# An attention and token-mixing MLP kernel: order of small loads, due phases of DVE steps, SBUF places and held pairs

## The chip, the core and the metric

The kernel runs on one core of one Trainium2 chip, as one launch. The core has TensorE (PE in the profile, its weight loads PEld), VectorE (DVE), ScalarE (ACT), GpSimd (POOL) and SyncE (SP), which issues the kernel's DMAs from one queue in program order. The metric is the time of one execution on the device in microseconds, as a median of several runs.

## The reference

`x` is 2048 rows (S) of 512 (D), everything in fp32. Two branches are mixed row by row with a gate:

```python
def _A_ref(x, wqkv, wo):                 # attention, H = 32 heads of Dh = 16
    qkv = (x @ wqkv).reshape(B, S, 3, H, Dh).transpose(2, 0, 3, 1, 4)
    q, k, v = qkv[0], qkv[1], qkv[2]
    p = softmax(einsum("bhqd,bhkd->bhqk", q, k) * Dh ** -0.5, axis=-1)
    o = einsum("bhqk,bhkd->bhqd", p, v)
    return o.transpose(0, 2, 1, 3).reshape(B, S, D) @ wo

def _B_ref(x, w1, b1, w2, b2):           # MLP across the tokens, F = 1792
    h = layernorm(x)
    u = gelu(einsum("bsd,sf->bdf", h, w1) + b1)
    return (einsum("bdf,fs->bds", u, w2) + b2).transpose(0, 2, 1)

g = sigmoid((x * gate_w).sum(-1, keepdims=True))
return g * _A_ref(...) + (1 - g) * _B_ref(...)
```

## The kernel before

**Stages.** Dense products are made in split precision: each fp32 operand becomes a high and a low part, and three matmuls (hi x hi, hi x lo, lo x hi) are added. The v, q and k projections come first, then the MLP's first layer (`layer`, with `gelu` on DVE and ACT; its last step is L438, `u_lo<-gu`). From about 305 us on runs the attention loop, whose instructions on all five engines stand in the order in which the code gives them (`manual_schedule`). A short end stage finishes the output projection.

**The loop.** There are 32 groups: 2 halves of the queries by 16 pairs of heads. Each group has four phases (`PHASES`), 128 in all, numbered `p`; `ph` is the phase within its group. A phase has 16 score matmuls (L876) on 64 rows of the TensorE array, into PSUM banks named s (one bank) or t (two). Between them, on the other 64 rows, stand up to 14 matmuls of dense work (L885): the MLP's second layer in groups 0 to 22, then the output projection of the first query half and parts of the second half's. Four scores are copied by DVE to an SBUF tile `pe` (L893), which ACT exponentiates at once at the end of the phase (L913). Six are exponentiated singly from PSUM (L897, tiles `p1`) and six as three pairs of banks (L906, tiles `p2` with four buffers). Then follow the av matmuls (L776, `apply_v`), which multiply the exps by v and, in the same matmuls, by a column that makes the softmax denominators r. DVE copies or adds their result to the group's tile `ot` (L798 add, L800 copy) and so frees the av bank.

**Held pairs.** The 16 exps of a phase are used in pairs: six in `TURNS`, the last of them (14, 15), and two in `HELD`, the `pe` pairs, whose av matmuls are made in the next phase. In `ph` 0, the previous group's held pairs come first and close that group: `store` sends its o (L765) and r (L767) to DRAM with four DMAs each. Also in `ph` 0, under a condition on which query blocks the turns cover, the pair (14, 15) is held over too. The condition is there because the result in `ot` can be added for one head or for both, but not for half of one.

**Order of the small work in a phase.** At the head of a phase, SP issues the next group's queries in `ph` 0 (`load_q`, 8 DMAs of 64 KB, L502) and keys in `ph` 1 (`load_k`, 6 DMAs of 128 KB, L502). After them come the entries of `calls` for that phase, and DVE steps recorded in `later` run after the phase's evacuations and before its `ot` addition (L923). What goes through `calls` and `later`:

- `invert(half, k, pairs, at)`: four groups fill one 128-row block k of the attention output. In the phase after their last store it loads the block's denominators (`inv<-r`, L615), takes maximum and reciprocal on DVE (L618, L619) in phase `at`, and writes them back in the next phase (`ri<-inv`, L623). The eight inversions lie in `ph` 1 of groups 4, 8, 12, 16, 20, 24, 28 and 31.
- `fetch_o(half, k, places, ats)`: loads block k of o (`e<-o`, L633) and its reciprocals spread over the rows of each head (`o_sum<-ri`, L634), and multiplies, copies the high part and subtracts for the low part on DVE, in the phases `ats`. `o_sum` has two buffers. The first half's four fetches are issued in phases 92, 92, 94 and 95 (group 23), the second half's first two in 99 and 102.
- `load_wo`, `load_wq`, and the loads of finished MLP rows (`row<-bp`).

**SBUF.** Places are given to pools from one side in the order in which they are opened: o, the stacks `stk` (two buffers of keys, two of queries), `ot` with the small tiles `inv`, `row` and `token`, then `pt` with the exps. A tile waits for the release of whatever lay there before; in the loop's first phases these are the MLP's tiles. In bytes of a partition the stacks begin at 69120 (where the normalized rows were), and `pt` at 104480.

Of the kernel before, what the change touches and what calls it, by code (L numbers as in the profile page):

```python
# [58 lines left out]
def gated_mix(ctx: ExitStack, tc: tile.TileContext, a_x, a_wqkv, a_wo, b_w1, b_b1, b_w2, b_b2, gate_w, out):  # L59
# [419 lines left out]
    o_pool = ctx.enter_context(tc.tile_pool(name="o", bufs=1, reuse_waits="tile"))  # L479
    att_ctx = ExitStack()  # L480
    stk = att_ctx.enter_context(tc.tile_pool(name="stk", bufs=2, reuse_waits="tile"))
    out_pool = att_ctx.enter_context(tc.tile_pool(name="ot", bufs=2, reuse_waits="tile"))
# [49 lines left out]
    ri_d = [[dram.tile([P // DH, QW], F32, name=f"ri{h}{k}") for k in range(ND)] for h in range(2)]  # L532
    ptp_ctx = ExitStack()
    ptp = ptp_ctx.enter_context(tc.tile_pool(name="pt", bufs=2, reuse_waits="tile"))
    psum_ctx = ExitStack()
# [28 lines left out]
    def call(at, *what):  # L564
        calls.setdefault(at, []).append(what)
# [31 lines left out]
    def place(n):  # L597
        return end.tile([P, QW], F32R, name=f"e{n}")

    def load_wq(at):  # L600
        wq.extend(place(n).rearrange("p (i c) -> p i c", i=2) for n in (4, 5))
        raw = end.tile([P, QW], F32, name="o_sum", bufs=2).rearrange("p (i c) -> p i c", i=2)
        nc.gpsimd.memset(raw, 0.0)
# [5 lines left out]

    def invert(half, k, pairs, at):  # L610

        n = pairs * 2
# [14 lines left out]
    def fetch_o(half, k, places, ats, pairs=4):  # L627

        n = pairs * 2
        rb = end.tile([P, QW], F32, name="o_sum", bufs=2)[: n * DH]  # L630
        hi, lo = (place(i)[: n * DH] for i in places)
# [74 lines left out]
    for half in range(2):  # L706
        for k in range(ND):
            pairs = 3 if half and k == ND - 1 else 4
            p0 = PHASES * (half * NP + 4 * k + pairs)
            call(p0 + 1, invert, half, k, pairs, p0 + 1)  # L710
    p0 = 2 * at
    call(p0, open_end)
    call(p0, fetch_o, 0, 0, (0, 1), (p0 + 1, p0 + 1, p0 + 1))
    call(p0, fetch_o, 0, 1, (2, 3), (p0 + 1, p0 + 2, p0 + 2))
    call(p0 + 2, fetch_o, 0, 2, (4, 5), (p0 + 2, p0 + 2, p0 + 3))
    call(p0 + 3, fetch_o, 0, 3, (6, 7), (p0 + 3, p0 + 3, p0 + 3))
    at += 2
    for t in range(NH):
        at = put_output(t, 3 * ND, at)
    p1 = PHASES * (NP + 2 * 4) + 3  # L720
    call(p1, fetch_o, 1, 0, (8, 9), (p1 + 1, p1 + 2, p1 + 2))
    call(p1 + 3, fetch_o, 1, 1, (10, 11), (p1 + 4, p1 + 5, p1 + 5))
    p2 = PHASES * (NP + 3 * 4) + 2
# [83 lines left out]
    with tc.manual_schedule(engines=engines):  # L807
# [11 lines left out]
        for p in range(LAST + 1):  # L819
            grp, ph = divmod(p, PHASES)  # L820
            second = ph % 2
            if ph == 0:
                at = [[0, 0], [0, 0]]
                if grp + 1 < NG:
                    qt[grp + 1] = load_q(grp + 1)
            if ph == 1 and grp + 1 < NG:
                kt[grp + 1] = load_k(grp + 1)
            for what, *args in calls.get(p, ()):
                what(*args)
            if not second:  # L830
# [94 lines left out]
            turns, now_held = ([tuple(units[n] for n in pair) for pair in pairs] for pairs in (TURNS, HELD))  # L925
            spare = share[2]
            if ph == 0:
                if held:
                    apply_v(av, grp - 1, held, final=True)
                    spare = share[3]  # L930
                    av = psum.tile([P, NB], F32, name=f"s{spare}")
                whole = {qb for pair in turns for i, _, qb, _ in pair if i}
                if len(whole) == 1:
                    now_held = now_held + turns[-1:]
                    turns = turns[:-1]
                apply_v(av, grp, turns)
# [11 lines left out]
    psum_ctx.close()  # L948

    ptp_ctx.close()  # L950


    with (
# [14 lines left out]

        parts, whole = place(6), end.tile([P, QW], F32, name="o_sum", bufs=2)
        sums, hi, lo = (column_halves(x) for x in (whole[:, :NB], parts[:, :NB], parts[:, NB:]))  # L970
# [140 lines left out]
```

## Time and profile before

| | us |
|---|---|
| runs: median (lowest to highest, 3 runs) | 1345.89 (1345.78 to 1346.16) |
| the profiled execution | 1346.58 |
| its span, from first to last instruction | 1344.8 |
| busy: PE / DVE / ACT / POOL | 1296.8 / 670.2 / 1094.2 / 178.6 |
| mean granted TensorE clock | 0.981 |

A row of the costliest groups reads: line, engine, operation, output<-input (partitions x elements, type) xcount, then busy us in all, mean ns of one, and after the second bar the idle time of that engine just before such an instruction with what ended most of it. A row of the list of waits reads: engine, tile and line that waits, <- what it waits for: us in total, times, longest. A row of the timeline reads: start, length, engine, line, operation, tile<-tiles, count, and in brackets the idle time before it with its releaser. "SPq" is the issuing of DMAs on SP. A run of equal instructions is one row with its count, and a window cuts such runs at its ends.

### The profile page before, as it was taken

The page shows a single profiled execution, that of the slowest core. Times are in us where ns is not written, and L with a number is a line of the kernel's source. Part 1 is how long each engine was busy: PE and PEld are TensorE (multiplying, and loading weights), DVE is VectorE, ACT ScalarE, POOL GpSimd, SP SyncE. Part 2 cuts the span into 40 slices and gives each one's busy share as a digit, 9 for nine tenths or more (in the row PEclk, how much of TensorE's full clock was granted, in tenths as well). Part 3 has the DMA queues.
Part 4 walks back from the last instruction along what each step waited for, and adds up shares of the span by engine and source line. Part 5 has one row for each costly group of instructions (what it writes and reads, how often), then busy time and mean ns, then how long its engine had stood idle before and what let it go on. Part 6 is the DMA issues. An engine that isn't in the chain of part 4 may idle for free.

```text
span 1344.8 us, 33141 instructions
## 1 busy us (share of the span) xinstructions
PE 1296.8 (96%) x13278; PEld 850.9 (63%) x13278; DVE 670.2 (50%) x1143; ACT 1094.2 (81%) x1537; POOL 178.6 (13%) x272
## 2 busy tenths in 40 slices
PE   9999999998999899999999999999999799998998
PEld 7888888875666566656656665666565356655554
DVE  5775471366444445444544453444444646454555
ACT  3453353358999899989989998999899789998994
POOL 0210344560111011101101101110110000000000
PEclk9999999999999899999999999999999899998999
DMA  3596633245343333424433333333224645333422
GB/s 127 155 319 259 221 100 99 87 102 107 78 90 77 74 74 79 88 51 88 84 64 67 76 72 59 78 86 80 59 53 95 136 97 120 83 86 85 84 45 77
DMA packets 92463, 133.20 MB, mean 99 GB/s; under 512 B 16182, under 2 KB 55244, under 8 KB 89229
## 3 DMA queue, kind: packets, MB, share of 16 engines
q1 hardware_dynamic: 91724, 129.94, 40.2%
q8 instruction: 108, 1.77, 0.6%
q10 hardware_dynamic: 576, 1.05, 0.2%
q14 instruction: 55, 0.44, 0.1%
HBM read 97.00 MB, written 33.93 MB: 97 GB/s over the span
## 4 chain that ended last, share of the span: by engine, by line
PE 82%; ACT 7%; DMA 5%; SPq 3%; issue 2%; DVE 1%; DVEq 0%; ACTq 0%
PE av L776 24%; PE s L876 18%; PE acc L416 11%; PE t L876 10%; PE acc L73 9%; PE s L776 4%; DMA inv<-r 3%; PE dn L885 3%; ACT p L897 2%; ACT p L906 2%; ACT pe L913 2%; SPq L502 1%; SPq L767 1%; DMA o_sum<-ri 1%; SPq L765 1%
## 5 line engine op out<-in xcount | busy, mean ns | idle before, releaser
L897 ACT ACTIVATE p<-s 128x512 f32<-128x512 f32 x768 | 397.5, 656 | 54.0 <-PE s L876 29.0
L876 PE MATMUL s<-qs,ks 64*128 64x512 f32 x1344 | 345.5, 408 | 35.3 <-DVE ot L800 17.1
L906 ACT ACTIVATE p<-t 128x1024 f32<-128x1024 f32 x352 | 349.8, 1139 | 0.4 <-PE t L876 0.2
L876 PEld LDWEIGHTS s<-qs,ks 64*128 64x128 f32 x1344 | 232.7, 186 | 140.5 <-issue 73.7
L893 DVE COPY pe<-s 128x512 f32<-128x512 f32 x512 | 317.7, 683 | 6.9 <-PE s L876 6.1
L776 PE MATMUL av<-p,v 128*32 128x256 f32 x4832 | 279.3, 380 | 0.0
L798 DVE TENSOR_TENSOR ot<-av,ot 128x512 f32<-128x512 f32 (+1 forms) x128 | 73.0, 571 | 386.7 <-PE av L776 386.6
L913 ACT ACTIVATE pe<-pe 128x2048 f32<-128x2048 f32 x129 | 260.8, 2024 | 0.0
L776 PEld LDWEIGHTS av<-p,v 128*32 128x32 f32 x4832 | 156.9, 111 | 106.6 <-issue 3.6
L876 PE MATMUL t<-qs,ks 64*128 64x512 f32 x704 | 189.4, 457 | 3.9 <-ACT p L897 0.2
L885 PE MATMUL dn<-u_lo,w_hi 64*128 64x512 f32 x430 | 177.7, 413 | 0.0
L885 PE MATMUL dn<-u_hi,w_lo 64*128 64x512 f32 x430 | 176.8, 411 | 0.0
L885 PE MATMUL dn<-u_hi,w_hi 64*128 64x512 f32 x428 | 175.5, 410 | 0.0
L66 POOL TENSOR_TENSOR w_lo<-w_raw,w_hi 128x512 fp32r<-128x512 f32 (+1 forms) x126 | 148.7, 1187 | 124.5 <-ACT w_hi L65 107.8
L876 PEld LDWEIGHTS t<-qs,ks 64*128 64x128 f32 x704 | 98.0, 190 | 86.7 <-ACT p L897 78.3
L776 PE MATMUL av<-pe,v 128*32 128x256 f32 x2048 | 144.0, 400 | 0.3 <-ACT pe L913 0.3
L889 POOL MEMSET token<- 1x1 f32 x124 | 11.4, 92 | 920.5 <-PE dn L885 791.6
L65 ACT CAST w_hi<-w_raw 128x512 fp32r<-128x512 f32 (+1 forms) x67 | 38.1, 569 | 79.6 <-PE acc L416 58.7
L776 PEld LDWEIGHTS av<-pe,v 128*32 128x32 f32 x2048 | 54.9, 112 | 60.7 <-ACT p L897 25.1
L416 PE MATMUL acc<-h_hi,w_hi 128*128 128x512 f32 x224 | 87.1, 389 | 0.0
L416 PE MATMUL acc<-h_lo,w_hi 128*128 128x512 f32 x224 | 87.1, 389 | 0.0
L416 PE MATMUL acc<-h_hi,w_lo 128*128 128x512 f32 x224 | 87.1, 389 | 0.0
(148 smaller groups left out, 1514.6 us busy)
## 6 DMA issues: line engine op xcount, KB each, us to landing
w_raw<-in_B_w_dram SPq DMA_DIRECT2D x96, 256.0 KB
ks<-kp SPq DMA_DIRECT2D x192, 128.0 KB
qs<-qp SPq DMA_DIRECT2D x256, 64.0 KB
qp<-pc SPq DMA_DIRECT2D x16, 768.0 KB
x<-in_A_x_dram SPq DMA_DIRECT2D x32, 256.0 KB
kp<-pc SPq DMA_DIRECT2D x16, 512.0 KB
w_raw<-in_B_w_dram SPq DMA_DIRECT2D x32, 128.0 KB
bp<-row SPq DMA_DIRECT2D x16, 256.0 KB
```

Of the source, the lines that this page charges most:

```text
L65: copy(hi, src)
L66: return sub(lo, src, hi.bitcast(F32), ALU.subtract)
L73: nc.tensor.matmul(ps, a, b, start=start and n == 0, stop=stop and n == last)
L416: nc.tensor.matmul(p, a, b, start=first and k == 0, stop=last and k == 2)
L776: nc.tensor.matmul(av[32 * j : 32 * (j + 1), i * QC : (i + 1) * QC], v_flat[:, v_at : v_at + 32], pt[:, h * QC : (h + 1) * QC], start=n == ...
L798: nc.vector.tensor_tensor(x, y, x, ALU.add)
L876: nc.tensor.matmul(s, kt[grp][rows_i, c * P : (c + 1) * P], qt[grp][rows_i, qb * NB : (qb + 1) * NB], start=True, stop=True,)
L885: mm = nc.tensor.matmul(ps, a[half], b[half], start=begin and not second, stop=last and bool(second))
L893: nc.vector.tensor_copy(pt, s)
L897: nc.scalar.activation(pt, s, AF.Exp, scale=SCALE)
L906: nc.scalar.activation(pt, twos[low, low + 1], AF.Exp, scale=SCALE)
L913: nc.scalar.activation(x, x, AF.Exp, scale=SCALE)
```

## The change

- `calls` of a phase are made at its head, ahead of `load_q` and `load_k`; before, they came after them.
- `invert`'s load stays in the same phase, and its DVE steps and the write back come two phases later, except for the second half's blocks 2 and 3 (groups 28 and 31).
- All four fetches of the first half are issued in phase 92; `o_sum` has three buffers. Their DVE phases stay. The second half's first two are issued in phases 99 and 103 (99 and 102 before), their DVE steps in 101, 102, 102 and 105, 106, 106 (100, 101, 101 and 103, 104, 104 before).
- The pool `pt` is opened ahead of `stk` and `ot`. In bytes of a partition `pt` now begins at 69120, the stacks at 114176 (keys 114176 and 122368, queries 130560 and 134656), and `ot` at 138752. In the first layer the bytes 130816 to 139008 held the gelu tiles `gu` and `gs`.
- In every phase but the last of a group, the pair (14, 15) is held over to the next phase, if the pairs that remain (with the held ones of the phase before, outside `ph` 0) cover both query blocks of each head that they touch.

```diff
--- before.py
+++ after.py
@@ -478,6 +478,7 @@
     bp_d = [dram.tile([P, D], F32, name=f"bp{t}") for t in range(NS)]
     o_pool = ctx.enter_context(tc.tile_pool(name="o", bufs=1, reuse_waits="tile"))
     att_ctx = ExitStack()
+    ptp = att_ctx.enter_context(tc.tile_pool(name="pt", bufs=2, reuse_waits="tile"))
     stk = att_ctx.enter_context(tc.tile_pool(name="stk", bufs=2, reuse_waits="tile"))
     out_pool = att_ctx.enter_context(tc.tile_pool(name="ot", bufs=2, reuse_waits="tile"))
     QW = 2 * NB
@@ -530,8 +531,6 @@
     o_d = [[dram.tile([P, QW], F32, name=f"o{h}{k}") for k in range(ND)] for h in range(2)]
     r_d = [[dram.tile([P // DH, QW], F32, name=f"r{h}{k}") for k in range(ND)] for h in range(2)]
     ri_d = [[dram.tile([P // DH, QW], F32, name=f"ri{h}{k}") for k in range(ND)] for h in range(2)]
-    ptp_ctx = ExitStack()
-    ptp = ptp_ctx.enter_context(tc.tile_pool(name="pt", bufs=2, reuse_waits="tile"))
     psum_ctx = ExitStack()
     ps_dn = psum_ctx.enter_context(tc.tile_pool(name="ps_dn", bufs=1, space=PSUM, reuse_waits="tile"))
     o_parts = {}
@@ -599,7 +598,7 @@
 
     def load_wq(at):
         wq.extend(place(n).rearrange("p (i c) -> p i c", i=2) for n in (4, 5))
-        raw = end.tile([P, QW], F32, name="o_sum", bufs=2).rearrange("p (i c) -> p i c", i=2)
+        raw = end.tile([P, QW], F32, name="o_sum", bufs=3).rearrange("p (i c) -> p i c", i=2)
         nc.gpsimd.memset(raw, 0.0)
         for j in range(4):
             nc.sync.dma_start(
@@ -609,6 +608,7 @@
 
     def invert(half, k, pairs, at):
 
+
         n = pairs * 2
         w = QW // DH
         t = out_pool.tile([P, w], F32, name="inv")[: n * DH]
@@ -627,7 +627,7 @@
     def fetch_o(half, k, places, ats, pairs=4):
 
         n = pairs * 2
-        rb = end.tile([P, QW], F32, name="o_sum", bufs=2)[: n * DH]
+        rb = end.tile([P, QW], F32, name="o_sum", bufs=3)[: n * DH]
         hi, lo = (place(i)[: n * DH] for i in places)
         raw = lo.bitcast(F32)
         nc.sync.dma_start(raw, o_d[half][k][: n * DH])
@@ -706,20 +706,20 @@
     for half in range(2):
         for k in range(ND):
             pairs = 3 if half and k == ND - 1 else 4
-            p0 = PHASES * (half * NP + 4 * k + pairs)
-            call(p0 + 1, invert, half, k, pairs, p0 + 1)
+            p0 = PHASES * (half * NP + 4 * k + pairs) + 1
+            call(p0, invert, half, k, pairs, p0 + (0 if half and k > 1 else 2))
     p0 = 2 * at
     call(p0, open_end)
     call(p0, fetch_o, 0, 0, (0, 1), (p0 + 1, p0 + 1, p0 + 1))
     call(p0, fetch_o, 0, 1, (2, 3), (p0 + 1, p0 + 2, p0 + 2))
-    call(p0 + 2, fetch_o, 0, 2, (4, 5), (p0 + 2, p0 + 2, p0 + 3))
-    call(p0 + 3, fetch_o, 0, 3, (6, 7), (p0 + 3, p0 + 3, p0 + 3))
+    call(p0, fetch_o, 0, 2, (4, 5), (p0 + 2, p0 + 2, p0 + 3))
+    call(p0, fetch_o, 0, 3, (6, 7), (p0 + 3, p0 + 3, p0 + 3))
     at += 2
     for t in range(NH):
         at = put_output(t, 3 * ND, at)
     p1 = PHASES * (NP + 2 * 4) + 3
-    call(p1, fetch_o, 1, 0, (8, 9), (p1 + 1, p1 + 2, p1 + 2))
-    call(p1 + 3, fetch_o, 1, 1, (10, 11), (p1 + 4, p1 + 5, p1 + 5))
+    call(p1, fetch_o, 1, 0, (8, 9), (p1 + 2, p1 + 3, p1 + 3))
+    call(p1 + 4, fetch_o, 1, 1, (10, 11), (p1 + 6, p1 + 7, p1 + 7))
     p2 = PHASES * (NP + 3 * 4) + 2
     assert p2 > 2 * at
     call(p2, fetch_o, 1, 2, (0, 1), (p2 + 1, p2 + 1, p2 + 1))
@@ -819,14 +819,14 @@
         for p in range(LAST + 1):
             grp, ph = divmod(p, PHASES)
             second = ph % 2
+            for what, *args in calls.get(p, ()):
+                what(*args)
             if ph == 0:
                 at = [[0, 0], [0, 0]]
                 if grp + 1 < NG:
                     qt[grp + 1] = load_q(grp + 1)
             if ph == 1 and grp + 1 < NG:
                 kt[grp + 1] = load_k(grp + 1)
-            for what, *args in calls.get(p, ()):
-                what(*args)
             if not second:
                 beside = [step(*args) for step, *args in dense.get(p // 2, ())]
             n_b = len(beside)
@@ -924,15 +924,20 @@
 
             turns, now_held = ([tuple(units[n] for n in pair) for pair in pairs] for pairs in (TURNS, HELD))
             spare = share[2]
+            if ph < PHASES - 1:
+
+                def whole(pairs):
+                    met = {(i, qb) for pair in pairs for i, _, qb, _ in pair}
+                    return all(len([1 for i, _ in met if i == n]) != 1 for n in range(2))
+
+                if whole(turns[:-1] + (held if ph else [])):
+                    now_held = now_held + turns[-1:]
+                    turns = turns[:-1]
             if ph == 0:
                 if held:
                     apply_v(av, grp - 1, held, final=True)
                     spare = share[3]
                     av = psum.tile([P, NB], F32, name=f"s{spare}")
-                whole = {qb for pair in turns for i, _, qb, _ in pair if i}
-                if len(whole) == 1:
-                    now_held = now_held + turns[-1:]
-                    turns = turns[:-1]
                 apply_v(av, grp, turns)
             elif p < LAST:
                 apply_v(av, grp, held + turns)
@@ -947,8 +952,6 @@
                 assert at == [[NS, NS], [NS, NS]]
     psum_ctx.close()
 
-    ptp_ctx.close()
-
 
     with (
         tc.tile_pool(name="ps_end", bufs=1, space=PSUM, reuse_waits="tile") as ps_end,
@@ -966,7 +969,7 @@
                 for i, (a, b) in mms[m:n]:
                     nc.tensor.matmul(pa[t], a, b, start=i == 0 and t not in LATE, stop=i == len(mms) - 1 and t in LATE)
 
-        parts, whole = place(6), end.tile([P, QW], F32, name="o_sum", bufs=2)
+        parts, whole = place(6), end.tile([P, QW], F32, name="o_sum", bufs=3)
         sums, hi, lo = (column_halves(x) for x in (whole[:, :NB], parts[:, :NB], parts[:, NB:]))
         last = column_halves(last_ot)
         totals = [column_halves(pa[t])[0] for t in (5, 7)]
```

## The prediction

> **What bounds the kernel now.** I read the totals and the chain of waits first, then the list of waits, then the timeline and the windows of the stages concerned. The page:
>
> ```profile
> span 1344.8 us, 33141 instructions
> ...
> PE av L776 24%; PE s L876 18%; PE acc L416 11%; PE t L876 10%; PE acc L73 9%; PE s L776 4%; DMA inv<-r 3%; PE dn L885 3%; ACT p L897 2%; ACT p L906 2%; ACT pe L913 2%; SPq L502 1%; SPq L767 1%; DMA o_sum<-ri 1%; SPq L765 1%
> ...
> L897 ACT ACTIVATE p<-s 128x512 f32<-128x512 f32 x768 | 397.5, 656 | 54.0 <-PE s L876 29.0
> L906 ACT ACTIVATE p<-t 128x1024 f32<-128x1024 f32 x352 | 349.8, 1139 | 0.4 <-PE t L876 0.2
> ```
>
> The chain is TensorE's scores and av matmuls, with two small loads in it, inv<-r (3%) and o_sum<-ri (1%). ScalarE's idle time stands in front of each phase's first exp (L897): 54.0 us in all. No repair of stalls in the loop can be worth much more than that. The list of waits names what is late:
>
> ```profile
> DVE ot L798 <- PE av L776: 386.6, 116, 6.2
> ...
> DVE inv L618 <- DMA inv<-r: 52.2, 8, 8.4
> ...
> DVE o_sum L923 <- DMA o_sum<-ri: 9.2, 1, 9.2
> ...
> DVE w_hi L65 <- DMA w_raw<-in_B_w_dram: 4.1, 1, 4.1
> ...
> PE s L876 <- DMA qs<-qp: 2.6, 1, 2.6
> ```
>
> Undisturbed, the loop has a law, which I read from the chain in order of time (start, us, what; the x72 and x64 rows are a phase's av matmuls, each program matmul shown twice) and from two exps of the steady stretch:
>
> ```profile
> 381.59 4.09 PE av L776 x72
> ...
> 411.82 4.08 PE av L776 x72
> ...
> 983.58 4.09 PE av L776 x72
> ...
> 1150.32 3.59 PE av L776 x64
> ...
> 1157.80 3.59 PE av L776 x64
> ```
>
> ```profile
> 376.50 2.10 ACT L913 ACTIVATE pe<-pe 128x2048 f32<-128x2048 f32 x1
> ...
> 383.87 2.20 ACT L913 ACTIVATE pe<-pe 128x2048 f32<-128x2048 f32 x1
> ```
>
> A phase with 64 av rows takes 1157.80-1150.32 = 7.48 us, 3.89 of it beside the av's own 3.59. A group of the first half, which has one 72-row and one 56-row phase, takes 411.82-381.59 = 30.23. A phase followed at 383.87-376.50 = 7.37 is as short as ScalarE lets it be: its exps fill it. In the windows view (PE, PEld, DVE, ACT, POOL busy, granted clock, DMA share, GB/s) the steady stretch is full on both engines and at clock 1.00:
>
> ```profile
> 306.00:318.00 12.00, 9.90 (x82) 6.15 (x82) 7.51 (x10) 8.57 (x13) 0.09 (x1) 0.86 1.01 189
> 446.00:458.00 12.00, 8.10 (x66) 5.28 (x66) 4.77 (x10) 7.23 (x11) 0.09 (x1) 0.72 0.28 46
> 460.00:565.00 105.00, 105.00 (x1304) 65.40 (x1308) 51.55 (x91) 104.15 (x144) 11.64 (x23) 1.00 0.38 81
> ```
>
> So what the change can win lies in the stalls, and the steady phases change only through their av counts.
>
> **Term 1, the inversions: -38.0.** The first stall, at group 4:
>
> ```profile
> 440.65 2.72 SPq L502 DMA_DIRECT2D ks<-kp  x6
> ...
> 443.89 0.43 SPq L615 DMA_DIRECT2D inv<-r  x1
> ...
> 450.09 0.20 DVE L618 TENSOR_SCALAR inv<-inv 128x64 f32<-128x64 f32 x1 [8.37 <-DMA inv<-r]
> ...
> 450.79 0.36 DVE L798 TENSOR_TENSOR ot<-av,ot 128x256 f32<-128x256 f32 x1
> ```
>
> The 32 KB load goes out behind six 128 KB key loads and lands 450.09-443.89 = 6.2 us later. VectorE stands 8.37 us at L618, and behind it on that engine stands the ot addition that frees the av bank; the next scores wait for that. The window 446 to 458 shows the wake: clock 0.72. The last inversion has no keys in front of it, and shows the load by itself:
>
> ```profile
> 1304.95 0.32 SPq L615 DMA_DIRECT2D inv<-r  x1
> ...
> 1306.65 0.19 DVE L618 TENSOR_SCALAR inv<-inv 96x64 f32<-96x64 f32 x1 [1.04 <-DMA inv<-r]
> ```
>
> Alone it takes 1306.65-1304.95 = 1.70 us. In the changed order the load stands behind the group's eight stores and ahead of the keys. VectorE's two steps come two phases (15 us) later for six of the eight; for groups 28 and 31 they stay in the same phase, where 1.7 us is about the cover that group 31 already has. What one stall costs the loop: the rows 411.82 and 983.58 are the same phase of groups 3 and 21, 18 groups and five stalls apart, and 571.76 - 18 x 30.23 = 27.6, or 5.5 each. The seventh, at group 28, lies between two ScalarE rows:
>
> ```profile
> 1212.49 2.21 ACT L913 ACTIVATE pe<-pe 128x2048 f32<-128x2048 f32 x1
> ...
> 1232.93 2.00 ACT L913 ACTIVATE pe<-pe 128x2048 f32<-128x2048 f32 x1
> ```
>
> 20.44 us for two phases, less 2 x 7.48, is 5.5. The sixth is mixed with other waits; I count 5.0. Together 38.1, and 38.0 is taken. At most all of it goes. At least 38.0 - 7 x 0.70 = 33.1 goes, if the two DVE steps themselves (450.09 to 450.79) stayed on the path. I take the upper end, because in 116 phases the ot addition waits 386.6/116 = 3.3 us for TensorE, which covers 0.70. If that cover were gone, the 4.9 would come back.
>
> **Term 2, the first half's fetches: -8.5.** At phase 92 the changed kernel issues all four, with a third o_sum buffer; before, the last two go out in phases 94 and 95:
>
> ```profile
> 1047.56 1.23 DVE L923 TENSOR_TENSOR e<-o_sum,e 128x1024 fp32r<-128x1024 f32 x1
> ...
> 1048.68 2.81 SPq L502 DMA_DIRECT2D ks<-kp  x6
> ...
> 1054.93 0.63 SPq L634 DMA_DIRECT2D o_sum<-ri  x1
> ...
> 1064.09 1.23 DVE L923 TENSOR_TENSOR o_sum<-e,o_sum 128x1024 f32<-128x1024 f32 x1 [9.19 <-DMA o_sum<-ri]
> ...
> 1067.59 1.68 ACT L897 ACTIVATE p<-s 128x512 f32<-128x512 f32 x3 [8.03 <-PE s L876]
> ...
> 1074.73 3.05 ACT L897 ACTIVATE p<-s 128x512 f32<-128x512 f32 x6 [0.92 <-PE s L876]
> ```
>
> ```profile
> 1052.05 11.95 DMA o_sum<-ri
> ```
>
> The chain has the third broadcast for 11.95 us, VectorE waits 9.19 for it, and ScalarE loses 8.03 + 0.92 = 8.95 in two phases. Fetched at 92, it has some 20 us, and the wait goes. What is late next: the fourth broadcast needs the first fetch's o_sum buffer, free at 1047.56 + 1.23 = 1048.8, and SP stands at it. Queued behind it are the queries of group 24, the eight stores of group 23 and the keys of group 24, which went out at 1048.68 and are wanted by the scores of phase 96 (1074.73 before, some 1066 after). Eight query issues (0.6 each, 4.17 for seven below), eight stores (the same each) and 2.81 for the keys make 12.4, so the last key leaves at 1061.2, and by the 6.2 that the load behind keys took it lands at 1067: about a microsecond late, of which I count 0.45. So -8.95 + 0.45 = -8.5. Bounds: -10.8, if the smaller waits around phase 93 go too (twice 0.92), and -3, if the keys are late by what rival A below works out. The second half's fetches move by a phase or two and have no idle in front of their steps in the list of waits: nothing. The changed order of DVE's steps there costs nothing: the same instructions, under the same 3.3 us of cover.
>
> **Term 3, the start of the loop: +3.5.** The p and pe tiles and the key and query stacks change places. The first queries now lie where the last gelu tiles were:
>
> ```profile
> 299.45 6.06 SPq L502 DMA_DIRECT2D qs<-qp  x8
> ...
> 304.64 0.68 DVE L438 TENSOR_TENSOR u_lo<-gu,u_hi 128x512 fp32r<-128x512 f32 x1
> ...
> 307.23 0.76 PE L876 MATMUL s<-qs,ks 64*128 64x512 f32 x1 [2.56 <-DMA qs<-qp]
> 307.31 4.17 SPq L502 DMA_DIRECT2D qs<-qp  x7
> ...
> 309.41 0.43 DVE L65 CAST w_hi<-w_raw 128x512 fp32r<-128x512 f32 x1 [4.09 <-DMA w_raw<-in_B_w_dram]
> ```
>
> Before, their eight loads begin at 299.45 and the first score at 307.23, 1.72 after the last issue ends. After, they wait for the gelu's last step, 304.64 + 0.68 = 305.32. At 0.47 per issue (the fastest that eight could go by the keys' row, 2.81 for six, 0.47 each) the last leaves at 309.1 and the score runs at 310.8, +3.6; at 0.60 (4.17 for seven) at 311.8, +4.6; at 0.76 (6.06 for eight) at 313.1, +5.9. Behind these issues stands the w_raw load for which VectorE's w_hi waits 4.09 before the first evacuations; it is pushed by the same 3.5 or so. Zero is the other end, if the new place comes free earlier than I read. I take +3.5, by the fast issue, because the keys, which shared the DMA engines with the queries before, now go earlier and are done. The window 306 to 318 shows clock 0.86 after a wait of 2.56 us: 0.14 x 12 = 1.7 us lost. A longer wait loses between nothing and that much more; I add none.
>
> The Trainium skill, page "TensorE: Matmul & The Clock Gate", section "Part 1: The HAM clock gate (the "warmup" mystery)", says that TensorE falls to half rate after an idle window of about 3.4 us and needs about as long a busy one to come back. The trace agrees in kind: 0.72 after the 3.90 us stand at group 4 against 0.86 after 2.56. By that rule the longer stand at the start, 2.56 + 3.5, would surely hold a whole window, and the sum would be about 1.7 higher, an estimate from that page.
>
> **Term 4, the held pairs: +2.5.** The program's av matmuls per phase, counted from the code, go in groups 0 to 22 from 28/36/32/32 to 28/32/32/36: the same four lengths, so nothing. Groups 23 and 28 to 31 go from four of 32 to 28/32/32/36, 24 to 27 to 32/28/32/36. A group with a short and a long phase takes 30.23 by the steady rows, one of four equal phases 4 x 7.48 = 29.92: +0.31 for eight of these nine groups (the last one's closing phase carries the end's matmuls either way), as the short phase cannot go below ScalarE's 7.37 and the long one pays in full. Bounds: +3.5 (by the law with its floor, 7.37 + 2 x 7.48 + 7.98 - 29.92 = 0.39, for nine groups) and -9.3 - 2.5 under rival C. The matmuls, exps and additions are as many as before.
>
> **Sum.** Against the profiled execution's 1346.58 us (its span 1344.8 and 1.8 around it): 1346.58 - 38.0 - 8.5 + 3.5 + 2.5 = 1306.1. The median of the runs shown, 1345.89, is 0.7 lower, so 1305.4.
>
> **The rivals.**
>
> A. The keys of group 24 come late in earnest. If the fourth broadcast takes the 11.95 us that the third took, and the last query load waits for it in SP's queue, then stores and keys follow from 1048.8 + 11.95 = 1060.8: 0.6 x 8 + 2.81 more, the last key lands near 1072 to 1074 in place of 1067, and term 2 loses 5 to 6. For it: the row 11.95. Against: that one had 768 KB of keys ahead of it (1048.68, then 1052.05), the new one has none. 1310.9.
>
> B. The start does not move, because the issue order or an earlier release makes up for the gelu wait. For it: VectorE waited 4.09 and TensorE 2.56 there already, so there is slack between the two. Against: both hang on the same SP queue. 1305.4 - 3.5 = 1301.9.
>
> C. Holding loosens the phases: with the last pair out of the way the long phase no longer pays its extra eight rows, and every group takes 29.92. Then groups 1 to 22 win 22 x 0.31 = 6.8 and term 4's 2.5 falls away: 1296.1. For it: ScalarE's floor is 7.37. Against: in the steady window TensorE is busy 105.00 of 105.00 us and ScalarE 104.15, so at most 0.85 per 105 us is to be had, 5.4 over 22 groups.
>
> D. The other side: the held pair's p tile is read one phase later, and the two-bank exp that takes that buffer next (L906) waits for it. ScalarE is full, so each such wait moves the loop. Newly held phases number 69 (three in 28 groups and two in four, 92, less 23 held before). At one exp's 1.139 us each that is 79 us: 1384. It decides from 40.5/69 = 0.59 us a phase. Against: in the 23 groups that held before, L906's idle time is 0.4 us in all.
>
> E. The change does not do what it says: the six moved inversions stall as before, because the small load still lands late or its steps stand behind other work. 6 x 5.4 comes back: 1337.8. Against: the row 1304.95, 1.70 us alone.
>
> **How the numbers follow.** Forecast 55%, A 16, B 12, C 10, D 4, E 3. The predicted time is 1305.4. The terms' bounds give 1299.6 (start 0, fetches -10.8) to 1318.9 (inversions -33.1, fetches -3, start +5.9, pairs +3.5, all at once). The range 1295 to 1312 takes in A, B and C and leaves out D, E and the upper bounds that would all have to fall together. About 0.2% (2.7 us) is what can be told from no change here. Only D ends above the old time, 0.04; no case lies within the bound but a mixture of D at its point, 0.01; faster 0.95.
>
> **What will show it.** DVE's wait for inv<-r falls from 52.2 to under 2 and the row leaves the chain; L897's idle falls from 54.0 to about 15. The o_sum wait of 9.19 is gone and the first scores of phase 96 wait for ks under 2 us (more is A). The first score comes at 310.8 (307.23 is B). Phase lengths over a group read about 7.4, 7.5, 7.5, 8.0 (four of 7.48 is C). L906's idle stays near 0.4 (tens of us is D). I am wrong if an inv wait of several microseconds is left, or if a new wait of one queue fills phases that ran full before.

## The result, and the profile after

The changed kernel takes 1310.64 us (median of four runs, 1309.61 to 1312.42), the kernel before 1346.03 beside it: a ratio of 0.9737, interval 0.972 to 0.9754. The forecast was 1305.4. The time lies inside the range, 5.2 us above the forecast and 0.3 from what rival A gave (1310.9). The profiled execution took 1312.42, the slowest of the four, its span 1310.3.

The page of the changed kernel, with the lines that answer to those shown of before:

```profile
span 1310.3 us, 33092 instructions
...
PE 1284.9 (98%) x13278; PEld 843.3 (64%) x13278; DVE 670.3 (51%) x1143; ACT 1092.3 (83%) x1537; POOL 178.8 (14%) x272
...
PE av L776 27%; PE s L876 21%; PE acc L416 12%; PE t L876 11%; PE acc L73 10%; PE s L776 5%; PE dn L885 2%; ACT p L897 2%; ACT p L906 2%; ACT pe L913 1%; DMA o_sum<-ri 1%; PE pa L970 1%; DVE pe L893 1%; PE acc L187 1%; PE acc L254 0%
...
L897 ACT ACTIVATE p<-s 128x512 f32<-128x512 f32 x768 | 406.5, 728 | 20.6 <-PE s L876 14.0
...
L906 ACT ACTIVATE p<-t 128x1024 f32<-128x1024 f32 x352 | 358.5, 1217 | 0.1
```

The work is the same (as many matmuls, DVE and ACT instructions); the inversions' load has left the chain, and ScalarE's idle time ahead of the phases fell from 54.0 to 20.6 us. The saving in that one number, 33.4, is nearly the whole 34.5 that the span is shorter. The list of waits shows what went, what grew and what is new:

```profile
DVE w_hi L65 <- DMA w_raw<-in_B_w_dram: 8.0, 1, 8.0
...
PE s L876 <- issue: 5.3, 1, 5.3
PE s L876 <- DMA qs<-qp: 4.6, 1, 4.6
...
DVE inv L618 <- DMA inv<-r: 4.2, 2, 2.6
...
DVE o_sum L923 <- DMA o_sum<-ri: 1.2, 1, 1.2
```

VectorE's waits for inv<-r fell from 52.2 to 4.2 (only groups 28 and 31 are left), and its wait for o_sum<-ri from 9.2 to 1.2. The two waits at the start grew from 4.1 and 2.6, and TensorE has a new wait of 5.3.

A table of the starts of some phases' first score matmul in both traces gives the account by stage; the last column is what the stage added or saved.

| first score of phase | before | after | difference | since the row above |
|---|---|---|---|---|
| 0 (group 0) | 307.23 | 309.88 | +2.65 | +2.65 |
| 12 (group 3) | 400.58 | 404.96 | +4.38 | +1.73, the start |
| 88 (group 22) | 1002.58 | 979.58 | -23.00 | -27.38, five inversions |
| 97 (group 24) | 1081.62 | 1054.60 | -27.02 | -4.02, the fetches and phase 92 |
| 100 (group 25) | 1108.91 | 1077.50 | -31.41 | -4.39, the sixth inversion |
| 112 (group 28) | 1198.79 | 1168.16 | -30.63 | +0.78, three groups with held pairs |
| 116 (group 29) | 1234.24 | 1198.74 | -35.50 | -4.87, the seventh inversion |
| 126 (group 31) | 1309.12 | 1274.03 | -35.09 | +0.41 |
| end of the span | 1344.8 | 1310.3 | -34.5 | +0.6 |

Two rows need care. Of the -4.02, 2.05 lie in phase 92 itself, which took 9.61 us before and 7.56 after, at another clock (last section). And a second profile of the changed kernel (the first experiment below) gives -7.21 in that row and +3.82 for the start: one profile does not fix these two terms.

**Where the missing microseconds are: phase 96.** The chain of the changed kernel in order of time (start, us, what), and the timeline of the same stretch:

```profile
1023.72 11.69 DMA o_sum<-ri
...
1035.42 0.31 SPq L503
```

```profile
1024.43 11.31 SPq L503 DMA_DIRECT2D qs<-qp  x8
...
1040.09 2.71 SPq L503 DMA_DIRECT2D ks<-kp  x6
...
1045.55 0.76 PE L876 MATMUL s<-qs,ks 64*128 64x512 f32 x1 [5.34 <-issue]
```

The fourth broadcast takes 11.69 us, and as it lands (1035.41) SP issues the last of the eight queries, which had stood behind it. In this trace SP's issues use eight completion semaphores in turn, and an issue waits for the DMA that had its semaphore before, eight places ahead of it. The first five queries go out by 1026.7; the last three start at 1029.58, 1031.98 and 1035.42, each 0.01 to 0.02 us after such a DMA has landed: the third broadcast, the fourth load of o and the fourth broadcast. The eight took 11.31 us of issuing; 3.55 is the row for eight such loads at the start of this kernel's loop (below). Then come the eight stores and, at 1040.09, the keys of group 24. TensorE stands 5.34 us for them: what A described. The row names no releaser ("issue"), but in the trace TensorE's own wait for a key load's semaphore ends at 1045.38, 0.04 us after the third of the six key loads has landed.

**The start.** The same rows as before, and the window of the first 12 us of the loop (columns as before: PE, PEld, DVE, ACT, POOL busy, clock, DMA share, GB/s):

```profile
305.30 0.68 DVE L438 TENSOR_TENSOR u_lo<-gu,u_hi 128x512 fp32r<-128x512 f32 x1
306.00 3.55 SPq L503 DMA_DIRECT2D qs<-qp  x8
...
309.88 0.76 PE L876 MATMUL s<-qs,ks 64*128 64x512 f32 x1 [4.55 <-DMA qs<-qp]
...
313.97 0.43 DVE L65 CAST w_hi<-w_raw 128x512 fp32r<-128x512 f32 x1 [7.99 <-DMA w_raw<-in_B_w_dram]
...
315.85 0.60 PE L876 MATMUL s<-qs,ks 64*128 64x512 f32 x1 [2.57 <-DVE pe L893]
```

```profile
309.00:321.00 12.00, 8.55 (x66) 5.64 (x70) 5.99 (x8) 6.83 (x11) 0.09 (x1) 0.72 0.76 178
```

The queries go out 0.02 us after the last gelu step ends (305.30 + 0.68 = 305.98). The weights that VectorE splits next are pushed by more, 309.41 to 313.97, and the clock in the window is 0.72 in place of 0.86. VectorE's first evacuations come behind these weights, and for them TensorE stands a second time, 2.57 us. Before, that second stand was short:

```profile
311.29 0.49 PE L876 MATMUL s<-qs,ks 64*128 64x512 f32 x1 [0.64 <-DVE pe L893]
```

The windows of phases 0 and 1, before and after:

```profile
307.23:324.94 17.71, 16.82 (x172) 9.82 (x172) 11.00 (x15) 15.51 (x21) 1.46 (x3) 0.92 0.75 152
```

```profile
309.88:329.07 19.19, 16.62 (x164) 10.36 (x164) 11.00 (x15) 14.90 (x21) 1.46 (x3) 0.84 0.64 141
```

TensorE is busy about as long as before (the held pairs move eight of the matmuls counted here to a later phase) and idle for 2.57 us in place of 0.89: the time that these phases add is for the most part the second stand.

### The profile page after: what moved, and what is told of

The parts are those of the page before. It is cut to its first block, busy times and chain, and to the rows that moved or that the text cites. A ratio compares the mean times of both kernels' runs of the same rounds, so it can differ in the third digit from the quotient of the medians.

```text
span 1310.3 us, 33092 instructions
## 1 busy us (share of the span) xinstructions
PE 1284.9 (98%) x13278; PEld 843.3 (64%) x13278; DVE 670.3 (51%) x1143; ACT 1092.3 (83%) x1537; POOL 178.8 (14%) x272
## 4 chain that ended last, share of the span: by engine, by line
PE 89%; ACT 5%; DMA 2%; DVE 2%; issue 1%; SPq 1%; ACTq 0%; DVEq 0%
PE av L776 27%; PE s L876 21%; PE acc L416 12%; PE t L876 11%; PE acc L73 10%; PE s L776 5%; PE dn L885 2%; ACT p L897 2%; ACT p L906 2%; ACT pe L913 1%; DMA o_sum<-ri 1%; PE pa L970 1%; DVE pe L893 1%; PE acc L187 1%; PE acc L254 0%
## 5 line engine op out<-in xcount | busy, mean ns | idle before, releaser
L897 ACT ACTIVATE p<-s 128x512 f32<-128x512 f32 x768 | 406.5, 728 | 20.6 <-PE s L876 14.0
L906 ACT ACTIVATE p<-t 128x1024 f32<-128x1024 f32 x352 | 358.5, 1217 | 0.1
L893 DVE COPY pe<-s 128x512 f32<-128x512 f32 x512 | 318.2, 683 | 13.5 <-PE s L876 12.4
L913 ACT ACTIVATE pe<-pe 128x2048 f32<-128x2048 f32 x129 | 269.7, 2094 | 0.0
L876 PE MATMUL t<-qs,ks 64*128 64x512 f32 x704 | 183.6, 447 | 2.9 <-DVE pe L893 0.8
L876 PEld LDWEIGHTS t<-qs,ks 64*128 64x128 f32 x704 | 91.5, 184 | 89.6 <-ACT p L897 86.3
L776 PE MATMUL av<-pe,v 128*32 128x256 f32 x2048 | 137.2, 385 | 0.1
```

What stands on the lines that cost most here:

```text
L776: nc.tensor.matmul(av[32 * j : 32 * (j + 1), i * QC : (i + 1) * QC], v_flat[:, v_at : v_at + 32], pt[:, h * QC : (h + 1) * QC], start=n == ...
L876: nc.tensor.matmul(s, kt[grp][rows_i, c * P : (c + 1) * P], qt[grp][rows_i, qb * NB : (qb + 1) * NB], start=True, stop=True,)
L893: nc.vector.tensor_copy(pt, s)
L897: nc.scalar.activation(pt, s, AF.Exp, scale=SCALE)
L906: nc.scalar.activation(pt, twos[low, low + 1], AF.Exp, scale=SCALE)
L913: nc.scalar.activation(x, x, AF.Exp, scale=SCALE)
```

## The experiments

Each was run five times, in three sets of four, with the kernel before run nine times beside each set. In the three sets the kernel before had a median of 1346.16, 1346.56 and 1347.39; across sets I compare by the ratio to it. The changed kernel, run again in the first set, is at 0.9733, so "the changed kernel" in the second and third set is 0.9733 x 1346.56 = 1310.6 and 0.9733 x 1347.39 = 1311.4.

**The changed kernel again.**

> The changed kernel itself, as the neighbour of the three runs beside it: 1310.6, within 1309.6 to 1312.4 as in its first four runs.

Measured: 1310.22 (1309.49 to 1312.57), ratio 0.9733 (0.972 to 0.9747). In its profile the eight queries take 8.19 us to issue in place of 11.31, and TensorE's wait at phase 96 is 2.6 us in place of 5.3. Five of the kernels below keep this order of issues in phase 92 (the queries first, the old rule, both of the inversions, the old places), and there the wait is 2.7 to 3.0: the first profile shows an unusually long one.

**The fourth fetch two phases later.**

```diff
-    call(p0, fetch_o, 0, 3, (6, 7), (p0 + 3, p0 + 3, p0 + 3))
+    call(p0 + 2, fetch_o, 0, 3, (6, 7), (p0 + 3, p0 + 3, p0 + 3))
```

> The changed kernel with the first half's fourth fetch issued in phase 94 in place of 92, nothing else. Theory (SP stands at the fourth broadcast and at the query loads behind it, so stores and keys of group 24 go out late): the issue of the eight queries shrinks from 11.31 us to under 6, TensorE's wait of 5.34 us at the start of phase 96 falls below 1, and the time falls by 4 to 6 us. Rival (the DMA engines are simply full from phase 92 on, whoever waits): the keys still come late or VectorE's wait for the fourth broadcast takes their place, and the time changes by less than 1.5 us.

Measured: 1317.38 (1316.91 to 1320.85), 7.2 slower than the changed kernel. Of the theory's three numbers one was met, the wait at phase 96. The timeline of this kernel:

```profile
1010.01 17.20 SPq L503 DMA_DIRECT2D qs<-qp  x8
...
1031.58 2.72 SPq L503 DMA_DIRECT2D ks<-kp  x6
...
1048.07 1.23 DVE L923 TENSOR_TENSOR o_sum<-e,o_sum 128x1024 f32<-128x1024 f32 x1 [11.96 <-DMA o_sum<-ri]
...
1051.94 0.79 PE L876 MATMUL s<-qs,ks 64*128 64x512 f32 x1 [10.61 <-DVE ot L798]
```

The keys did leave 8.5 us earlier (1031.58 in place of 1040.09), and phase 96 began without a wait. But the fourth broadcast now followed 768 KB of keys; VectorE waited 11.96 us for it, and TensorE 10.61 behind VectorE: the stall of the kernel before, moved by one fetch. And the queries' issue did not shrink, it grew to 17.20, so the fourth broadcast had not been their only obstacle: they stood behind the first three as well. Moving this one fetch could not settle it, because the queries and the broadcast stand in each other's way.

**Queries ahead of keys in the pool.** The first queries then lie on bytes that were free long before, the second group's keys on the gelu tiles.

```diff
+    q_bufs = [stk.tile([P, QW], F32R, name=f"qs{i}", bufs=1) for i in range(2)]
     k_bufs = [stk.tile([P, S], F32R, name=f"ks{i}", bufs=1) for i in range(2)]
...
-        t = stk.tile([P, QW], F32R, name="qs")
+        t = q_bufs[g % 2]
```

> The changed kernel with the two query buffers laid ahead of the two key buffers in the same pool, so that the first queries no longer lie on the last gelu tiles (the second group's keys do). Theory (the first queries wait for the last gelu step): they are issued at 298 to 300 in place of 306.0, the first score runs at 307 or earlier in place of 309.88, and the time falls by 2.5 to 4.5 us. Rival (the weights loaded behind them set the start): VectorE's wait of 8.0 us for w_raw stays above 6 and the time falls by less than 1.

Measured: 1304.69 (1303.27 to 1306.43), 5.5 faster; ratio 0.9689 (0.9676 to 0.9702). The theory holds, and its size was taken too small. The w_raw load that the rival names stands behind the queries in the queue and came early with them, so this run does not tell the two apart. Rows of its timeline, and its windows of the loop's first 12 us and of phase 92:

```profile
298.41 5.51 SPq L504 DMA_DIRECT2D qs<-qp  x8
...
305.27 0.49 PE L877 MATMUL s<-qs,ks 64*128 64x512 f32 x1
...
306.77 0.43 DVE L65 CAST w_hi<-w_raw 128x512 fp32r<-128x512 f32 x1 [0.80 <-PE s L877]
```

```profile
305.00:317.00 12.00, 10.49 (x95) 5.91 (x94) 10.12 (x15) 9.96 (x17) 0.09 (x1) 1.00 0.91 187
1002.00:1012.00 10.00, 9.28 (x90) 4.19 (x80) 4.21 (x11) 8.82 (x12) 0.00 (x0) 0.83 0.95 210
```

The first score runs without a wait and 2 us earlier than even in the kernel before, whose keys and queries went out at 296.71 and 299.45; the weights are there too, and the clock stays at 1.00. So the new places did help the keys, which went out at 295.08, and only the queries' place was bad. Group 3 begins at 397.77, 7.2 earlier than in the changed kernel; phase 92 gives 1.5 of that back (last section).

**The old rule for held pairs.**

```diff
-            if ph < PHASES - 1:
...
-                if whole(turns[:-1] + (held if ph else [])):
-                    now_held = now_held + turns[-1:]
-                    turns = turns[:-1]
...
+                whole = {qb for pair in turns for i, _, qb, _ in pair if i}
+                if len(whole) == 1:
+                    now_held = now_held + turns[-1:]
+                    turns = turns[:-1]
```

> The changed kernel with the old rule for held pairs. Theory (held pairs move eight rows from one phase to another; only groups 23 to 31 lose, by ScalarE's floor in the short phase): 0.26 for each of eight groups and about 0.5 at the end, so 2 to 3 us faster, with groups 1 to 22 at 30.23 as before. Rival (holding loosens the phases): slower, by up to 7 us over groups 1 to 22.

Measured: 1309.3 (1308.28 to 1313.56), 0.9 faster, with intervals that overlap (0.9711 to 0.9744 against 0.972 to 0.9747). The total is below the 2 to 3 expected and does not decide; the trace does. From phase 100 to 104 a group took 29.94 us here and 30.22 in the changed kernel: 0.28, as the theory says. In groups of the first half it is 30.2 to 30.4 in both, and groups 1 to 22 together took 635.4 us here and 635.1 in the changed kernel: the rival's loss of up to 7 us is not there.

**The inversions' loads behind the keys again.** `invert` is called after `load_k`, all else as changed.

```diff
             for what, *args in calls.get(p, ()):
-                what(*args)
+                if what is not invert:
+                    what(*args)
...
                 kt[grp + 1] = load_k(grp + 1)
+            for what, *args in calls.get(p, ()):
+                if what is invert:
+                    what(*args)
```

> The changed kernel with the loads of the inversions put back behind the phase's key loads; the DVE steps stay two phases later (in the same phase for groups 28 and 31). Theory (either the two phases or the place ahead of the keys is enough): the six moved inversions still wait for nothing, only group 28 stalls again, 4.5 to 5.5 us more than the changed kernel. Rival (the place in the queue is what counts): all seven stall, some 33 to 38 us more.

Measured: 1315.99 (1312.66 to 1319.27), 5.4 slower by the ratio, 0.977 (0.9746 to 0.9794).

**The inversions' DVE steps in the phase of their loads.**

```diff
-            call(p0, invert, half, k, pairs, p0 + (0 if half and k > 1 else 2))
+            call(p0, invert, half, k, pairs, p0)
```

> The changed kernel with all eight inversions' DVE steps in the phase of their loads, which stay ahead of the keys. Theory (either is enough): VectorE waits up to 2.8 us for each, as it does at groups 28 and 31 in the changed kernel, under the cover of its wait for TensorE; 0 to 2.5 us more than the changed kernel. Rival (the two phases are what counts): six stalls of about 5 us come back, 25 to 33 us more.

Measured: 1312.57 (1310.8 to 1314.9), 2.0 slower, ratio 0.9745 (0.9727 to 0.9763); the interval overlaps that of the changed kernel. The row of the list of waits in the former kernel and in this one:

```profile
DVE inv L618 <- DMA inv<-r: 8.8, 2, 7.4
```

```profile
DVE inv L618 <- DMA inv<-r: 16.4, 8, 4.8
```

With the loads behind the keys, one long wait is left, 7.4 us, at group 28, whose steps are not moved. With the steps in place, there are eight waits of 2 us on average, the longest 4.8 where up to 2.8 was expected, and only at group 4 (1.3 us by the starts of its phases) does one reach the loop. So either half of the edit removes the six stalls; the two phases do it wholly, and the place in the queue is what serves group 28.

**Reciprocals written twice.** The inverted block goes to DRAM with each row doubled, so that the broadcast has 16 rows to start from.

```diff
-    ri_d = [[dram.tile([P // DH, QW], F32, ...
+    ri_d = [[dram.tile([P // DH, 2, QW], F32, ...
-            nc.sync.dma_start(ri_d[half][k][:n].rearrange("r (a b) -> (r a) b", b=w), t)
+            for e in range(2):
+                nc.sync.dma_start(ri_d[half][k][:n, e].rearrange("r (a b) -> r a b", b=w), t)
-        nc.sync.dma_start(rb, ri_d[half][k][:n, None, :].broadcast_to([n, DH, QW]))
+        twice = ri_d[half][k][:n].rearrange("n e q -> (n e) q")
+        nc.sync.dma_start(rb, twice[:, None, :].broadcast_to([n * 2, DH // 2, QW]))
```

> The changed kernel with each row of reciprocals written back to DRAM twice (one more small DMA per inversion), so that a broadcast of them starts from 16 rows in place of 8. Theory (a broadcast from 8 rows keeps only part of the DMA engines at work, some 6 us each, and SP's issues wait for them one after the other): the broadcasts take about half as long, the eight query issues shrink from 11.31 us to under 8, TensorE's wait at the start of phase 96 goes, 3 to 6 us faster than the changed kernel. Rival (the bytes or packets are the limit, not the rows): same broadcasts, same wait, within 1 us.

Measured: 1304.64 (1303.73 to 1306.91), 6.0 faster; ratio 0.9693 (0.9674 to 0.9712). The busy share of the DMA engines from 1005 to 1040 us in 40 slices (tenths, as on the page), first in the changed kernel and then in this one:

```profile
DMA  0039776999999988455445587645565565203210
```

```profile
DMA  0099899999999999982000599999411019995997
```

In the changed kernel, from 1019 on, the mean share is about half for 16 us; that is the rest of the broadcasts running one after another. By the trace the four land at 1016.52, 1022.89, 1029.56 and 1035.41, some 6 us apart, so that much of the fourth's 11.69 us is waiting for the third. A broadcast from 8 rows moves its completion semaphore once at its issue and eight times at its end; from 16 rows it moves sixteen times at its end. With 16 rows the first three broadcasts are done by 1021.5, the engines are free when the fourth broadcast and the queries come, and the fourth takes 5.05. Rows of this kernel's timeline:

```profile
1023.97 4.75 SPq L503 DMA_DIRECT2D qs<-qp  x8
...
1033.04 2.71 SPq L503 DMA_DIRECT2D ks<-kp  x6
```

The eight query issues take 4.75 in place of 11.31, the keys leave 7 us earlier, and phase 96 starts without the wait. Phases 95 and 96 take 15.4 us together, against 22.4 and 19.2 in the two profiles of the changed kernel. The Trainium skill says this in "DMA: Bandwidth & Descriptors", section "Rules for kernel authors": an outermost dimension of fewer than 16 confines the DMA to at most that many engines. The trace agrees, by the share of about 0.5 and the eight steps of the semaphore for a broadcast from 8 rows.

**Both.**

> Both the queries' place of the second experiment and the doubled reciprocals. If the two act apart, their gains add: 5.5 and the gain of the doubled reciprocals alone, so 1299 to 1302 if that one is 3 to 6. If the broadcasts stay as long, 1304 to 1305.

Measured: 1298.11 (1297.71 to 1299.03), ratio 0.9642 (0.9624 to 0.9659): 12.5 faster than the changed kernel, where 5.5 and 6.0 make 11.5, and 0.9 below the band as written. They act apart. Phase 92 takes 7.55 us here, so the 1.5 lost there in the second experiment is not lost again.

**All three.**

> The queries' place, the doubled reciprocals and the old rule for held pairs together. By adding: 1298.1 of the two, less the 0.9 to 2 that the old rule gave: 1296 to 1297.5. If the held pairs gain something where the stalls are gone, 1298 or more.

Measured: 1296.46 (1295.43 to 1298.08), ratio 0.9625 (0.961 to 0.9639), the fastest version by its median, though its interval overlaps that of "Both": 15 us below the changed kernel and 51 below the one before. Its page:

```profile
span 1293.4 us, 33193 instructions
...
PE 97%; ACT 1%; DVE 1%; issue 0%; DVEq 0%; ACTq 0%
...
L900 ACT ACTIVATE p<-s 128x512 f32<-128x512 f32 x768 | 397.8, 674 | 6.0 <-PE s L879 1.9
```

ScalarE's idle time ahead of the phases is down to 6.0 us of the 54.0, and TensorE is 97% of the chain: no load has a share in it any more.

**The old places.** The pool of the exps is opened after the stacks, as before; the three o_sum buffers fit in either order.

```diff
-    ptp = att_ctx.enter_context(tc.tile_pool(name="pt", bufs=2, reuse_waits="tile"))
     stk = att_ctx.enter_context(tc.tile_pool(name="stk", bufs=2, reuse_waits="tile"))
...
+    ptp = ptp_ctx.enter_context(tc.tile_pool(name="pt", bufs=2, reuse_waits="tile"))
     psum_ctx = ExitStack()
```

> The changed kernel with the exps' pool opened after the stacks again, so all places as before, with three o_sum buffers. Theory (the new places only delay the first queries): the first score runs at 307 as before, groups 1 to 22 start 4 to 5 us earlier, 1305 to 1306.5. Rival (the old places made other loads wait, which the new ones free): less than 2 us faster, or slower.

Measured: 1307.17 (1306.99 to 1307.64), 0.7 above the band as written, and 4.2 faster by the ratio, 0.9704 (0.9691 to 0.9717). The first score runs at 306.96, and group 3 begins at 400.10 in place of 404.96: 4.9 (4.3 against the second profile), and close to the 400.58 of the kernel before. The start's loss comes from the places alone.

**The inversions alone, in the kernel before.** The diff is the change's own line for `invert`, with its calls made ahead of the queries and keys and all other calls left behind them.

> The kernel before with the inversions' part alone: their loads ahead of queries and keys, their DVE steps two phases later as in the change. Theory (the inversions are nearly all of the gain): 36 to 38.5 us faster than the kernel before, VectorE's wait for inv<-r from 52 to under 6. Rival (part of the gain is only shifted to the fetches and the start): 25 to 33.

Measured: 1311.51 (1310.89 to 1311.99) against 1347.39, 35.9 faster; ratio 0.9734 (0.972 to 0.9747). That is 0.1 below the theory's band and above the rival's; the wait for inv<-r fell to 2.3. In its profile the stages with the seven inversions give -37.4, as in the changed kernel, and phases 88 to 97 lose 1.2. This part alone is worth as much as the whole change, within the spread: the others together come to nothing, the fetches' gain against the start and the pairs. The row that shows what it leaves in place:

```profile
DVE o_sum L927 <- DMA o_sum<-ri: 12.0, 3, 9.9
```

**The first half's fetches alone, in the kernel before.**

```diff
-    call(p0 + 2, fetch_o, 0, 2, (4, 5), (p0 + 2, p0 + 2, p0 + 3))
-    call(p0 + 3, fetch_o, 0, 3, (6, 7), (p0 + 3, p0 + 3, p0 + 3))
+    call(p0, fetch_o, 0, 2, (4, 5), (p0 + 2, p0 + 2, p0 + 3))
+    call(p0, fetch_o, 0, 3, (6, 7), (p0 + 3, p0 + 3, p0 + 3))
```

(and three `o_sum` buffers)

> The kernel before with the first half's four fetches issued in phase 92 and three o_sum buffers, nothing else. Theory (the stall at the third broadcast goes, and group 24's keys come late behind the fourth): 3 to 6 us faster, VectorE's wait of 9.2 gone, a wait of TensorE or ScalarE of 2.5 to 6 at the start of phase 96. Rival (the forecast's term): 8 to 9 us faster.

Measured: 1338.24 (1336.66 to 1341.15), 9.2 faster; ratio 0.9932 (0.9917 to 0.9948). My theory missed, and the forecast's term was right for this kernel; in its profiled execution, the slowest of the five, the gain is smaller, 6.7 us by the start of phase 97. Here `calls` still come after `load_q`:

```profile
1030.44 3.62 SPq L502 DMA_DIRECT2D qs<-qp  x8
...
1061.39 2.71 SPq L502 DMA_DIRECT2D ks<-kp  x6
```

With the queries ahead of the fetches they take 3.62 us to issue, the keys leave 27 us after the first fetch (1034.16 to 1061.39) in place of 33 (1006.88 to 1040.09 in the changed kernel), and phase 96 starts at 1067.44 with a wait of 0.4. This points to the `calls` ahead of the queries in phase 92 as what made the keys of the changed kernel late. That line alone, put back in the changed kernel, was not tried, so this is argued and not shown.

## Why the prediction was right, and where it was off

**Inversions: right.** Forecast -38.0; the table gives -27.38 for five, and -4.65 and -5.13 for the last two when 0.26 a group for the held pairs is taken out (0.78/3): -37.2. The part alone gave -35.9 in the kernel before. Both mechanisms that the forecast named, the load ahead of the keys and the later DVE steps, suffice by themselves for the six moved inversions (but for 1.3 us at group 4 where the steps stay), which the forecast did not tell apart. The cover of 3.3 us for VectorE's two steps held: without it only 33.1 would have gone.

**Fetches: the step that failed.** Forecast -8.5; measured -4.0 in the first profile and -7.2 in the second. The failing step is "Eight query issues (0.6 each, 4.17 for seven below), eight stores (the same each) and 2.81 for the keys make 12.4". The stores and keys went as said (4.3 and 2.71 in the first profile); the queries took 11.31 and 8.19 us in place of 4.8, because the last of them stood behind the broadcasts. Phases 95 and 96 then took 7.0 and 3.8 us more than the 15.4 that the doubled reciprocals leave, where the forecast counted 0.45 for late keys. Against this, 2.05 us were won in phase 92, which the forecast had only in its bound. Rival A had the place and the price of the broadcast (11.95, measured 11.69), and its loss of 5 to 6 us lies between those of the two profiles. I gave it 16% for a wrong reason: I held that the third broadcast was slow because of the keys ahead of it. The doubled rows show that a broadcast from 8 rows keeps the DMA engines' share at about half and that four of them land one after the other; the keys were only one of the things that such a queue can stand behind. That the median lies 0.3 us from A's number is luck in part, since the start and phase 92 were off too.

**Start: the size was off.** Forecast +3.5, measured +4.4 (second profile +3.8). The mechanism was as said, the wait for the last gelu step; the fast issue (3.55 for eight) was right too, and the first score came at +2.65, earlier than the +3.6 worked out for it. The failing step is that w_raw "is pushed by the same 3.5 or so": VectorE had it 4.56 us later, 1.9 more than the first score, and TensorE stood for the evacuations behind it, 2.57 us in place of 0.64. The clock ("I add none") fell from 0.86 to 0.72 in the first 12 us. That is the direction that the rule gives which the prediction cites from the Trainium skill, page "TensorE: Matmul & The Clock Gate", section "Part 1: The HAM clock gate (the "warmup" mystery)". Its price of 1.7 us is not shown: the longer second stand is by itself as large as the rest of the term, 1.73, and no run parts the two. "Surely" was too much as well: the first stand was 4.55 us and not 2.56 + 3.5, and the clock of the trace changes in steps of 3.41 us on a fixed grid, of which only a stand of twice that is sure to cover a whole one. With both stands shorter (queries first) the clock is 1.00 from the first score on.

**Held pairs: right.** Forecast +2.5; the table has 0.78 for three groups and some 2.3 for all, with the end. A run with the old rule shows 0.28 per group in its trace and 0.9 in its median, which by itself is not clear of the spread.

**Two sums.** The upper bounds of all terms together make 1319.2, not 1318.9 (1305.4 + 4.9 + 5.5 + 2.4 + 1.0), and under rival C term 4 would be -6.8, not "-9.3 - 2.5". The forecast and the range do not hang on either.

**The rivals and the signs.** A happened, in the mechanism. B fell (309.88). C fell: a group takes 30.22 with the short and the long phase, as before. D fell: L906's idle time is 0.1 us. E fell: the six moved inversions wait for nothing. Three of the signs missed: the wait for inv<-r is 4.2 and not under 2, in two waits at the unmoved inversions; L897's idle time is 20.6 and not about 15; and phase 96 waited 5.34 and not under 2. The last is the "new wait of one queue" that was named as a sign of being wrong, and so it was for term 2.

## What to carry to other kernels

When small loads are moved ahead in a queue that issues in order, price the issues that come behind them by the completion of the moved loads, not by the length of an issue; a stall at one load can come back at the next tenant of the same queue. Before moving a slow small load, ask why it is slow: giving the broadcast 16 rows to read from won 6.0 us, where issuing one of the four later lost 7.2. And when a pool moves, look for each tile's former tenant: the first load into the new place waits for the last step of whatever lay there.

## What the runs showed of the hardware

Phase 92 has no dense matmuls beside its scores. In the kernel before and in the experiment with the queries first, TensorE's granted clock in it was 0.83, although TensorE was busy for 9.27 and 9.28 of 10 us; in the changed kernel it was 1.00:

```profile
1010.00:1017.00 7.00, 6.28 (x68) 3.16 (x70) 3.97 (x10) 6.86 (x12) 0.00 (x0) 1.00 0.96 221
```

The phase took 9.07 us in the one experiment and 7.56 in the changed kernel: 1.5 us for a state that no wait of TensorE explains, and that I had not expected to differ between kernels with the same instructions there. In the experiment's trace it is a single interval of 3.41 us at a clock of 0.50:

```profile
1006.41:1009.82 3.41, 3.31 (x28) 1.49 (x30) 0.44 (x2) 3.41 (x5) 0.00 (x0) 0.50 0.98 235
```

The phase was as long, 9.23 and 9.24 us at a clock of 0.82, with the old places and with the inversions' steps in place. What sets it off is open. It is worth 1.5 us or more in some kernels and nothing in others, so differences of that size between two versions here need their clocks beside them.
